# Retention attention and two feed-forward stages on one core: other ways to spread 1/rms, column sums and two scalars, one table row moved, and the last store halved

## The chip, the core and the metric

The program runs on one core of a Trainium2 chip. The core has TensorE (PE, matrix products into PSUM), VectorE (DVE), ScalarE (ACT), GpSimd (POOL) and SyncE (SP, which here only issues DMAs). The metric is the device time of one execution, in microseconds. The kernel before took 584.2 us as the median of three runs (584.07 to 584.91).

## The reference

Three stages follow one another on 1536 tokens of 512 channels, all in float32:

```python
# 1: causal retention in 8 heads of 64 channels, decay lam[h], two sequences of 768 tokens
out = ((q k^T) * lam^(i-j)) v, carried from block to block in a 64x64 state
# 2: x (1536x512) -> h = x @ w_in (512x2048)
r = maximum(h, 0); g = s * r * r + b; x = g @ w_out        # w_out 2048x512, s and b are scalars
# 3: rms = sqrt(mean(x*x, axis=-1) + 1e-6); xn = x / rms * rms_g
g = xn @ w_gate; val = xn @ w_val                          # 512x1536 each
out = (silu(g) * val) @ w_out                              # 1536x512
```

## The kernel before

**Layout.** Tokens lie along the free dimension, in two blocks of 768 (s = 0 and 1, `BW`), channels on the 128 partitions. A float32 product is made of three products of rounded parts (`PASSES`: high by high, high by low, low by high); ACT writes a high part (L143) and DVE the low part, source minus high (L146).

**Order.** The order of each engine's instructions is the order of the code (`manual_schedule`): generators `hquad` and `quad` yield after each part of a unit, and a table `plan`, keyed by (unit, part), says which other work is issued there. Semaphores hold an instruction until its inputs are there, and an engine does not pass a waiting instruction.

**Stage 2, h.** Sixteen units, `hquad(0)` to `hquad(15)`. From unit 4 on a unit is seven products of six matmuls (a 2x2 scheme with seven products instead of eight), in four PSUM banks b0 to b3; units take turns with two sets of banks. The parts are: product into b0, ACT copies it out (L378); product into b1, DVE adds (L316); product into b2, DVE adds; product into b3, DVE adds; and last three more products that are accumulated onto b0, b2 and b3, each of which therefore waits until the earlier reader of its bank is done. In between, `w_tasks` prepares the weights of later units from raw words: `first` to `fourth` unpack (ACT L123 and L129, DVE shift L135 and sum L140) and POOL makes four sums (L220 to L223); `first_hi`, `first_lo`, `second_hi`, `second_lo` split them. The table rows `wt[6]` and `wt[7]` say in which parts of units 9 to 12 this is done.

**Stage 2, second product.** For each block 16 steps of a `y_product` (512 tokens, four channel groups, 12 matmuls) and a `z_product` (256 tokens, 12 matmuls). The bias b enters as b times the column sums of w_out: POOL adds the rows of w_out into `wsum` (L434), and in step 15 of block 0 TensorE sums `wsum` over partitions and spreads s and b from one row, both with plain float32 products into bank 3 (L864, L865). DVE makes `sg_col`, `bc_col`, `bg_col` from that (L866 to L869); ACT (`square`) and DVE (`take`) then read y and z out with them.

**1/rms.** `norm_rstd(s)` sums squares over channels with TensorE (`nps`, L766), DVE scales (L768), POOL takes the power -1/2 (L770) and splits the 128x6 result in two parts (L773, L774). `norm_apply` spreads it: 12 products of 128 columns whose weights are a column of a part repeated (L781) give a bank `rb` in which every partition holds 1/rms of its token, and `norm_scale` multiplies x by that (DVE, L795). For block 0 this stands in steps 1, 3 and 4 of block 1's y products, for block 1 in quads 0 and 1.

**Stage 3.** 24 units `quad(0)` to `quad(23)` like `hquad`, with ACT's Silu (L982, L989) and a product on DVE (L958); quads 0 to 3 are of block 0. Then `out_product` and `store`: 12 row tiles, copied out of PSUM by ACT (even) or DVE (odd) and sent by SP.

## Time and profile before

| | |
|---|---|
| median of three runs | 584.2 us (584.07 to 584.91) |
| the profiled execution | 584.34 us, span 582.6 us |
| granted TensorE clock | 0.999 |
| busy: PE, DVE, ACT, POOL | 575.9, 404.4, 319.9, 114.6 us |
| the chain that ended last | 95% PE, 2% DMA, 1% DVE, 1% ACT |
| stages on TensorE | attention to 43.6, h to 165.8, y and z to 303.4, quads to 481.0, out to 579.0 us |

Times in rows are microseconds from the first instruction of the profiled execution. A busy figure of PE includes the pipelined ends of matmuls, so the distance from one group's start to the next one's start is read as its cost. A bracket at a row's end gives the idle time before it on its engine and what ended it.

### The profile page before, as it was taken

To read this page: it belongs to the slowest core of one execution; us is meant where nothing else is said; L and a number is where in the kernel's file an instruction comes from. 1 tells how busy PE (TensorE), PEld (TensorE's weight loads), DVE (VectorE), ACT (ScalarE), POOL (GpSimd) and SP (SyncE) were. 2 spreads that over 40 slices of the span, in tenths; PEclk is the share of its full clock that TensorE was granted. 3 is DMA by queue.
4 is the path that set the end of the run, shared out by engine and by line. 5 is a ranking of instruction groups with operands and counts; after the bars stand their busy time and mean duration, and the time that the engine had idled before them with its cause. 6 is when DMAs were issued, how large, how long until landed. Compare 5 with 4: busy or idle time off the path is not lost.

```text
span 582.6 us, 9398 instructions
## 1 busy us (share of the span) xinstructions
PE 575.9 (99%) x3682; PEld 536.8 (92%) x3682; DVE 404.4 (69%) x642; ACT 319.9 (55%) x558; POOL 114.6 (20%) x129
## 2 busy tenths in 40 slices
PE   8999999999999999999999999999999999999997
PEld 7889999999998888888899999999999998888886
DVE  6688947777777774769847967777777777874200
ACT  3889977776876662537552434444444446763200
POOL 4660312212123330222211002222222200000000
PEclk9999999999999999999999999999999999999999
DMA  8972222222324330222110012222222213320300
GB/s 327 397 291 75 72 74 73 73 74 72 109 73 145 123 131 1 73 72 71 30 45 2 1 37 61 75 72 75 71 75 75 79 36 109 108 73 1 146 36 37
DMA packets 17283, 52.00 MB, mean 89 GB/s; under 512 B 2390, under 2 KB 2390, under 8 KB 17238
## 3 DMA queue, kind: packets, MB, share of 16 engines
q1 hardware_dynamic: 17232, 51.39, 25.7%
q8 instruction: 29, 0.48, 0.3%
q14 instruction: 16, 0.13, 0.1%
q10 hardware_dynamic: 6, 0.00, 0.0%
HBM read 48.24 MB, written 3.15 MB: 88 GB/s over the span
## 4 chain that ended last, share of the span: by engine, by line
PE 95%; DMA 2%; DVE 1%; ACT 1%; SPq 0%; issue 0%; DVEq 0%
PE q L305 30%; PE h L305 20%; PE out L1095 17%; PE y L806 15%; PE z L818 8%; PE o L581 2%; PE sc L527 2%; DMA k<-in_kT_dram 1%; DMA q<-in_qT_dram 1%; PE o L596 1%; PE st L591 1%; PE rb L781 0%; PE nps L766 0%; DVE u_None L140 0%; DVE u_None L135 0%; DVE xq_None L316 0%
## 5 line engine op out<-in xcount | busy, mean ns | idle before, releaser
L143 ACT ACTIVATE u_None<-u_None 128x768 fp32r<-128x768 f32 (+2 forms) x50 | 42.8, 870 | 51.8 <-DVE u_None L140 45.8
L305 PE MATMUL q<-u0b_None,u_None 128*128 128x384 f32 x360 | 68.0, 334 | 0.0
L305 PEld LDWEIGHTS q<-u0b_None,u_None 128*128 128x128 f32 x360 | 62.7, 188 | 0.0
L146 DVE TENSOR_TENSOR u_None<-u_None,u_None 128x512 fp32r<-128x512 f32 (+1 forms) x66 | 53.1, 829 | 11.1 <-ACT u_None L143 11.0
L220 POOL TENSOR_TENSOR u_None<-u_None 128x256 f32<-128x256 f32 x18 | 19.8, 1099 | 184.4 <-DVE u_None L140 184.4
L305 PE MATMUL q<-xs_None,u_None 128*128 128x384 f32 x288 | 55.2, 334 | 0.0
L123 ACT ACTIVATE u_None<-st_None 128x512 f32<-128x512 f32 x68 | 45.1, 664 | 17.6 <-issue 14.3
L140 DVE CUSTOM_DVE_ANT_0 u_None<-u_None 128x1024 uint16<-128x1024 uint16 x68 | 47.1, 693 | 5.7 <-ACT u_None L129 0.6
L305 PEld LDWEIGHTS q<-xs_None,u_None 128*128 128x128 f32 x288 | 50.4, 188 | 0.0
L129 ACT ACTIVATE u_None<-st_None 128x512 uint32<-128x512 uint16 x68 | 45.2, 664 | 5.1 <-DVE u_None L146 5.1
L316 DVE TENSOR_TENSOR st_None<-q,r_None 128x384 f32<-128x384 f32 x48 | 26.6, 554 | 19.1 <-PE q L305 19.1
L989 ACT ACTIVATE st_None<-r_None 128x384 f32<-128x384 f32 x24 | 12.6, 526 | 45.9 <-DVE r_None L316 43.3
L1095 PE MATMUL out<-u_None,xs_None 128*128 128x512 f32 x144 | 32.8, 389 | 0.0
L1095 PEld LDWEIGHTS out<-u_None,xs_None 128*128 128x128 f32 x144 | 27.0, 188 | 5.6
L135 DVE TENSOR_SCALAR u_None<-u_None 128x512 uint32<-128x512 uint32 x68 | 31.1, 457 | 1.2 <-ACT u_None L123 1.0
L1102 DVE COPY st_None<-out 128x512 f32<-128x512 f32 x4 | 2.8, 692 | 40.9 <-PE out L1095 40.9
L434 POOL TENSOR_TENSOR wsum_None<-wsum_None,u_None 128x512 f32<-128x512 f32 x15 | 20.6, 1373 | 47.8 <-DVE u_None L140 47.8
L305 PE MATMUL q<-u0a_None,u_None 128*128 128x384 f32 x144 | 28.8, 334 | 0.0
L305 PE MATMUL q<-g_None,u_None 128*128 128x384 f32 x144 | 26.9, 334 | 0.0
L1095 PE MATMUL out<-u_None,u0b_None 128*128 128x512 f32 x108 | 25.3, 389 | 0.0
L305 PEld LDWEIGHTS q<-u0a_None,u_None 128*128 128x128 f32 x144 | 25.3, 188 | 0.0
L305 PEld LDWEIGHTS q<-g_None,u_None 128*128 128x128 f32 x144 | 25.1, 188 | 0.0
(207 smaller groups left out, 1291.9 us busy)
## 6 DMA issues: line engine op xcount, KB each, us to landing
st_None<-in_w_dram SPq DMA_DIRECT2D x68, 512.0 KB, 3.3
kv<-in_kv_dram SPq DMA_DIRECT2D x12, 512.0 KB, 7.2
q<-in_qT_dram SPq DMA_DIRECT2D x12, 256.0 KB, 7.1
k<-in_kT_dram SPq DMA_DIRECT2D x12, 256.0 KB, 7.1
out_dram<-st_None SPq DMA_DIRECT2D x8, 256.0 KB, 2.0
out_dram<-u_None SPq DMA_DIRECT2D x4, 256.0 KB, 2.0
row<-in_lam_dram ACTq DMA_DIRECT2D x1, 0.0 KB
row<-in_s_dram ACTq DMA_DIRECT2D x1, 0.0 KB
```

Source lines behind the costliest of these rows:

```text
L123: nc.scalar.activation(m, t[:, :, 1].bitcast(F32), AF.Prelu, scale=2.0**-112, alpha=-(2.0**32))
L129: nc.scalar.activation(to.bitcast(U32), low, AF.Copy, scale=2.0**-13)
L135: nc.vector.tensor_scalar(m, m, 3, None, op0=ALU.logical_shift_left)
L140: nc.vector.tensor_tensor(m, m, t.bitcast(U32), op=ALU.add)
L143: nc.scalar.activation(to, src, AF.Copy)
L146: nc.vector.tensor_tensor(to, src, hi.bitcast(F32), op=ALU.subtract)
L305: nc.tensor.matmul(ps, ws[:, wi, wop * KC + kt * P : wop * KC + (kt + 1) * P], xs[xop][:, xi, kt, :], start=n == 0 and not more, stop=n == ...
L316: nc.vector.tensor_tensor(to, ps, more, op=ALU.add)
L434: nc.gpsimd.tensor_tensor(wsum, wsum, m, op=ALU.add)
L806: nc.tensor.matmul(acc[d], wt[:, wi, d * P : (d + 1) * P], gt[:, gi, 0:BT], start=it == 0 and pi == 0, stop=it == NF1 - 1 and pi == 2,)
L818: nc.tensor.matmul(acc2[d // 2][:, d % 2 * BX : (d % 2 + 1) * BX], wt[:, wi, d * P : (d + 1) * P], gt[:, gi, BT:BW], start=it == 0 and pi ...
L1095: nc.tensor.matmul(ps, rows_[:, ai], w_out[f][:, wi, :], start=first and pi == 0, stop=last and pi == 2)
```

## The change

- **Column sums of w_out.** `wsum` is split in two parts in step 13 of block 0 (ACT, DVE), two products of 512 columns with a matrix of ones (`ones_r`, made once by POOL) put the sums in bank 3 behind the z products of that step, ACT copies one row out of PSUM, and two DMAs on SP's queue take it to DRAM and back as 128x4 (`cs_col`), 512 pieces of 4 bytes. DVE reads that in step 15, behind the products.
- **s and b** are loaded by two DMAs on SP's queue that repeat the one value over 128 partitions, behind `g_col`'s; the two DMAs on ACT's queue and the small product go.
- **1/rms of block 0** goes to DRAM as one row (a DMA of 768 pieces of 4 bytes) and comes back repeated over 128 partitions into `m_r`, both on SP's queue; `norm_scale` reads SBUF. The 12 products go.
- **1/rms of block 1.** ACT (high part) and POOL (low part) multiply the unit matrix by 1/rms, which gives diagonal matrices of two tiles each; a product of `ones_r` and a diagonal spreads it. Six products of 256 columns in place of twelve of 128, in quad 1, and six scalings in place of four.
- **One unit of h** (`wt[6]`, and the first task of `wt[7]`) in other slots.
- **The last row tile** is stored in halves: ACT copies and sends one, DVE copies and SP sends the other.

In the table the rows of `wt[6]` and `wt[7]` change; the diff cut to its core:

```diff
+                nc.sync.dma_start(s_col, s.partition_broadcast(P))
+                nc.sync.dma_start(b_col, b.partition_broadcast(P))
+    ones_r = late.tile([P, P], F32R, name="ones_r")
+    nc.gpsimd.tensor_copy(ones_r, ones)
...
-        (wt[6], ((9, 4), (10, 1), (10, 2), (10, 2), (10, 3), (10, 4), (10, 4), (11, 0))),
-        (wt[7], ((11, 1), (11, 3), (11, 4), (11, 4), (12, 1), (12, 2), (12, 2), (12, 3))),
+        (wt[6], ((9, 4), (10, 1), (10, 2), (10, 3), (10, 3), (10, 4), (11, 0), (11, 1))),
+        (wt[7], ((11, 2), (11, 3), (11, 4), (11, 4), (12, 1), (12, 2), (12, 2), (12, 3))),
...
+        return rstd
+
+    def spread_by_memory(rstd):
+
+        row = dram.tile([BW], F32, name="rstd_row")
+        nc.sync.dma_start(row.rearrange("(t p) -> p t", p=P), rstd)
+        nc.sync.dma_start(m_r, row.partition_broadcast(P))
...
+    def diagonals(rstd):
+
+        parts = const.tile([P, 2, NTT], F32R, name="parts")
+        nc.gpsimd.tensor_copy(parts[:, 0], rstd)
+        nc.gpsimd.tensor_tensor(parts[:, 1], rstd, parts[:, 0].bitcast(F32), op=ALU.subtract)
+        for n in range(NTT // 2):
+            hi, lo = rooms[n % 2]
+            for t in range(2):
+                nc.scalar.activation(
+                    hi[:, t * P : (t + 1) * P], unit, AF.Copy, scale=parts[:, 0, 2 * n + t : 2 * n + t + 1].bitcast(F32)
+                )
+            nc.gpsimd.tensor_tensor(
+                lo.rearrange("p (t i) -> p t i", t=2),
+                unit.rearrange("p (o i) -> p o i", o=1).to_broadcast([P, 2, P]),
+                parts[:, 1, 2 * n : 2 * n + 2].bitcast(F32).rearrange("p (t o) -> p t o", o=1).to_broadcast([P, 2, P]),
+                op=ALU.mult,
+            )
+            yield hi, lo
+
+    def norm_apply(s, n, ps, d):
+
+        for i in range(2):
+            nc.tensor.matmul(ps[:, 0 : 2 * P], ones_r, d[i], start=i == 0, stop=i == 1)
+        norm_scale(s, slice(2 * n * P, 2 * (n + 1) * P), ps[:, 0 : 2 * P])
...
+            if m == NF1 - 3:
+                split_hi(wsum_parts[0], wsum)
+                split_lo(wsum_parts[1], wsum, wsum_parts[0])
...
+            if m == NF1 - 3:
+
+                cs = bank(3, "cs")
+                for i in range(2):
+                    nc.tensor.matmul(cs, ones_r, wsum_parts[i], start=i == 0, stop=i == 1)
+                nc.scalar.activation(wsum[0:1, :], cs[0:1, :], AF.Copy)
+                row = dram.tile([1, DM], F32, name="cs_row")
+                nc.sync.dma_start(row, wsum[0:1, :])
+                nc.sync.dma_start(cs_col, row.rearrange("o (d p) -> p (o d)", p=P))
+            if m == NF1 - 1:
+                nc.vector.tensor_scalar(sg_col, g_col, s_col, None, op0=ALU.mult)
+                nc.vector.tensor_scalar(bc_col, cs_col, b_col, None, op0=ALU.mult)
+                nc.vector.tensor_tensor(bg_col, bc_col, g_col, op=ALU.mult)
...
-                norm_rstd(0, bank(0, "nps0"))
+                spread_by_memory(norm_rstd(0, bank(0, "nps0")))
             if it in (3, 4):
-                h = it - 3
-                norm_apply(0, slice(h * HB, (h + 1) * HB), bank(1 - h, f"rb0_{h}")[:, 0:HB])()
+                cols = slice((it - 3) * HB, (it - 2) * HB)
+                norm_scale(0, cols, m_r[:, cols])
...
         product(b0, ws, xs, A12, B21, True)
+        while between:
+            between.pop()()
...
+    rows_of = {}
+
+    def rstd_1():
+        d = diagonals(norm_rstd(1, bank(1, "nps1")))
+        rows_of.update(zip(range(2), d))
+        rows_of[None] = d
+
+    def spread(n):
+        norm_apply(1, n, bank((2, 3, 1)[n], f"rb1_{n}"), rows_of[n])
...
-        (0, 4): [lambda: norm_rstd(1, bank(1, "nps1"))],
-        (1, 2): [spread],
-        (1, 3): [lambda: scale[1]()],
+        (0, 4): [rstd_1],
+        (1, 3): [
+            lambda: spread(0), lambda: spread(1), lambda: rows_of.update({2: next(rows_of[None])}),
+            lambda: between.append(lambda: spread(2)),
+        ],
...
+        if i == NT // P - 1:
+
+            for j, (buf, queue) in enumerate(((out_buf[0], nc.scalar), (to, nc.sync))):
+                c = slice(j * DM // 2, (j + 1) * DM // 2)
+                if j:
+                    nc.vector.tensor_copy(buf[:, c], ps[:, c])
+                else:
+                    nc.scalar.activation(buf[:, c], ps[:, c], AF.Copy)
+                queue.dma_start(out[i * P : (i + 1) * P, c], buf[:, c])
+            return
```

Three places where instructions stand elsewhere now. First VectorE in units 10 and 11 of h, before: `h_2`, `h_3` and `h_1` in a row are banks b2, b3 and b1 of a unit, L135 and L140 are the shift and the sum of the raw words, L146 the low parts.

```order
L316 TENSOR_TENSOR xq_5_None<-h_2_1527,r_None 128x384
L135 TENSOR_SCALAR u_2_None<-u_2_None 128x512
L140 ISA u_2_None<-u_2_None 128x1024
L316 TENSOR_TENSOR xq_5_None<-h_3_1528,xq_5_None 128x384
L316 TENSOR_TENSOR xq_5_None<-h_2_1527,r_None 128x384
L316 TENSOR_TENSOR xq_5_None<-h_3_1528,r_None 128x384
L405 TENSOR_SCALAR xq_5_None<-xq_5_None 128x384
L146 TENSOR_TENSOR u_3_None<-u_2_None,u_3_None 128x768
L146 TENSOR_TENSOR u_3_None<-u_2_None,u_3_None 128x512 x2
L316 TENSOR_TENSOR r_None<-h_1_1597,q_9_None 128x384
L316 TENSOR_TENSOR u_17_None<-h_2_1598,r_None 128x384
L316 TENSOR_TENSOR u_17_None<-h_3_1599,u_17_None 128x384
```

The same place now:

```order
L315 TENSOR_TENSOR xq_5_None<-h_2_1528,r_None 128x384
L135 TENSOR_SCALAR u_2_None<-u_2_None 128x512
L315 TENSOR_TENSOR xq_5_None<-h_3_1529,xq_5_None 128x384
L140 ISA u_2_None<-u_2_None 128x1024
L315 TENSOR_TENSOR xq_5_None<-h_2_1528,r_None 128x384
L315 TENSOR_TENSOR xq_5_None<-h_3_1529,r_None 128x384
L404 TENSOR_SCALAR xq_5_None<-xq_5_None 128x384
L146 TENSOR_TENSOR u_3_None<-u_2_None,u_3_None 128x768
L315 TENSOR_TENSOR r_None<-h_1_1597,q_9_None 128x384
L146 TENSOR_TENSOR u_3_None<-u_2_None,u_3_None 128x512 x2
L315 TENSOR_TENSOR u_17_None<-h_2_1598,r_None 128x384
L315 TENSOR_TENSOR u_17_None<-h_3_1599,u_17_None 128x384
```

The second sum stands behind the add that reads b3 of unit 10, and the pair of low parts (`second_lo`) has gone from ahead of the add that reads b1 of unit 11 to the place between it and the add that reads b2.

Second ScalarE at the turn from quad 0 to quad 1, before: `q_0_3046` is b0 of quad 0, `q_0_3120` b0 of quad 1; the copy of b0 (L967), its Silu (L982) and the Silu of the other half (L989).

```order
L982 ACTIVATE st_24_None<-q_0_3046 128x384
L989 ACTIVATE st_24_None<-r_None 128x384
L967 ACTIVATE st_24_None<-q_0_3120 128x384
L982 ACTIVATE st_24_None<-q_0_3120 128x384
L989 ACTIVATE st_24_None<-r_None 128x384
L143 ACTIVATE xs_None<-xq_6_None 128x768
```

The same place now, where L996 is the copy, L1013 and L1020 the two Silu:

```order
L1013 ACTIVATE st_24_None<-q_0_3038 128x384
L1020 ACTIVATE st_24_None<-r_None 128x384
L798 ACTIVATE wsum_None<-unit_r,parts 128x128 x2
L798 ACTIVATE u_22_None<-unit_r,parts 128x128 x2
L996 ACTIVATE st_24_None<-q_0_3119 128x384
L798 ACTIVATE wsum_None<-unit_r,parts 128x128 x2
L1013 ACTIVATE st_24_None<-q_0_3119 128x384
L1020 ACTIVATE st_24_None<-r_None 128x384
L143 ACTIVATE xs_None<-xq_6_None 128x768
```

Four of ACT's multiplications of the unit matrix stand ahead of the copy of quad 1's b0, and two behind it.

Third VectorE in quad 1, before: L316 are the adds, L146 low parts of weights, L795 the scalings of x.

```order
L316 TENSOR_TENSOR r_None<-q_1_3121,st_24_None 128x384
L146 TENSOR_TENSOR u_23_None<-u_2_None,u_23_None 128x512 x2
L316 TENSOR_TENSOR st_24_None<-q_2_3122,r_None 128x384
L795 TENSOR_TENSOR xq_6_None<-xq_6_None,rb_0_3149 128x2x384 x2
L316 TENSOR_TENSOR st_24_None<-q_3_3123,st_24_None 128x384
L795 TENSOR_TENSOR xq_6_None<-xq_6_None,rb_1_3156 128x2x384 x2
L316 TENSOR_TENSOR st_24_None<-q_2_3122,r_None 128x384
L316 TENSOR_TENSOR r_None<-q_3_3123,r_None 128x384
```

The same place now, with the scalings in L784:

```order
L315 TENSOR_TENSOR r_None<-q_1_3120,st_24_None 128x384
L146 TENSOR_TENSOR u_23_None<-u_2_None,u_23_None 128x512 x2
L315 TENSOR_TENSOR st_24_None<-q_2_3121,r_None 128x384
L315 TENSOR_TENSOR st_24_None<-q_3_3122,st_24_None 128x384
L784 TENSOR_TENSOR xq_6_None<-xq_6_None,rb_0_3155 128x2x256 x2
L784 TENSOR_TENSOR xq_6_None<-xq_6_None,rb_1_3160 128x2x256 x2
L784 TENSOR_TENSOR xq_6_None<-xq_6_None,rb_2_3174 128x2x256 x2
L315 TENSOR_TENSOR st_24_None<-q_2_3121,r_None 128x384
L315 TENSOR_TENSOR r_None<-q_3_3122,r_None 128x384
```

All scalings stand behind the add that reads b3 and ahead of the add that reads b2 for the second time (the last row but one shown starts with `st_24_None<-q_2`).

## Rows read from the trace of the kernel before

**Rows 1.** the page, part 4: shares of the chain that ended last.

```profile
PE 95%; DMA 2%; DVE 1%; ACT 1%; SPq 0%; issue 0%; DVEq 0%
```

**Rows 2.** stretch: PE, PEld, DVE, ACT, POOL busy us (instructions); clock, DMA share, GB/s.

```profile
317.00:324.00 7.00, 7.00 (x43) 7.00 (x42) 6.86 (x11) 2.13 (x4) 0.00 (x0) 1.00 0.00 1
```

**Rows 3.** the chain of waits: start us, us, what.

```profile
227.10 1.43 PE z L818 x12
229.63 2.94 PE y L806 x12
...
250.66 1.43 PE z L818 x12
252.70 2.80 PE y L806 x12
...
315.35 1.29 PE rb L781 x12
```

**Rows 4.** POOL timeline, 214 to 262: start us, us, instruction, idle before and releaser.

```profile
243.88 1.46 POOL L770 TENSOR_TENSOR rstd<-ms,neg_half 128x6 f32<-128x6 f32 x1 [24.43 <-DVE ms L768]
```

**Rows 5.** DMA issues: what, KB each, median us from issue to landing.

```profile
st_None<-in_w_dram SPq DMA_DIRECT2D x68, 512.0 KB, 3.3
...
g_col<-in_rms_g_dram SPq DMA_DIRECT2D x1, 2.0 KB, 4.9
```

**Rows 6.** TensorE timeline, 104 to 146.

```profile
126.17 1.25 PE L305 MATMUL h<-u0a_None,st_None 128*128 128x384 f32 x6
128.09 1.32 PE L305 MATMUL h<-u0b_None,st_None 128*128 128x384 f32 x6 [0.67 <-DVE xq_None L316]
129.25 1.21 PE L305 MATMUL h<-xs_None,st_None 128*128 128x384 f32 x6
...
134.46 1.20 PE L305 MATMUL h<-wm_None,st_None 128*128 128x384 f32 x6
```

**Rows 7.** VectorE timeline, 104 to 146.

```profile
125.96 0.78 DVE L135 TENSOR_SCALAR u_None<-u_None 128x512 uint32<-128x512 uint32 x1
126.88 0.69 DVE L140 CUSTOM_DVE_ANT_0 u_None<-u_None 128x1024 uint16<-128x1024 uint16 x1
```

**Rows 8.** ScalarE timeline, 104 to 146.

```profile
127.60 0.85 ACT L143 ACTIVATE u_None<-u_None 128x768 fp32r<-128x768 f32 x1 [1.82 <-DVE u_None L140]
...
130.34 1.04 ACT L143 ACTIVATE u_None<-u_None 128x1024 fp32r<-128x1024 f32 x1
131.29 0.47 ACT L378 ACTIVATE q_None<-h 128x384 f32<-128x384 f32 x1
...
132.40 0.66 ACT L123 ACTIVATE u_None<-st_None 128x512 f32<-128x512 f32 x1
```

**Rows 9.** POOL timeline, 296 to 336.

```profile
314.46 0.19 POOL L773 CAST parts<-rstd 128x6 fp32r<-128x6 f32 x1
```

**Rows 10.** ScalarE groups by shape: count, busy us, mean ns, idle before.

```profile
L550 ACT ACTIVATE kdec<-kv,dec 128x64 f32<-128x64 f32 x40 | 10.6, 336 | 7.1 <-DMA kv<-in_kv_dram 7.0
...
L603 ACT ACTIVATE xq_None<-o 128x256 f32<-128x256 f32 x12 | 4.4, 370 | 3.1 <-PE o L596 3.1
```

**Rows 11.** VectorE timeline, 296 to 336.

```profile
314.42 0.56 DVE L316 TENSOR_TENSOR r_None<-q,st_None 128x384 f32<-128x384 f32 x1 [1.23 <-PE q L305]
314.89 1.28 DVE L146 TENSOR_TENSOR u_None<-u_None,u_None 128x512 fp32r<-128x512 f32 x2
...
321.13 0.56 DVE L316 TENSOR_TENSOR r_None<-q,r_None 128x384 f32<-128x384 f32 x1
...
326.13 0.55 DVE L316 TENSOR_TENSOR st_None<-q,st_None 128x384 f32<-128x384 f32 x1
```

**Rows 12.** POOL timeline, 104 to 146.

```profile
125.72 0.74 POOL L220 TENSOR_TENSOR u_None<-u_None 128x256 f32<-128x256 f32 x1 [10.24 <-DVE u_None L140]
```

**Rows 13.** TensorE timeline, 326 to 372.

```profile
326.94 3.28 PE L305 MATMUL q<-u0b_None,u_None 128*128 128x384 f32 x18
```

**Rows 14.** VectorE timeline, 540 to 584.

```profile
579.02 0.69 DVE L1102 COPY st_None<-out 128x512 f32<-128x512 f32 x1 [15.63 <-PE out L1095]
```

More of the change, by code (lines that the diff above doesn't have):

```diff
@@ L150, in attention_moe_moe2_kernel @@
     params = const.tile([P, H], F32, name="params")
-    row2 = const.tile([1, 2], F32, name="row2")
     params2 = const.tile([P, 2], F32, name="params2")
@@ L759, in norm_total @@
         norm_pair(s, 0)
-    rstd_parts = {}
+    dram = ctx.enter_context(tc.tile_pool(name="dram", bufs=1, space=bass.MemoryType.DRAM))
     def norm_rstd(s, ps):
@@ L795, in norm_scale @@
             nc.vector.tensor_tensor(y, y, by, op=ALU.mult)
+    def diagonals(rstd):
+        parts = const.tile([P, 2, NTT], F32R, name="parts")
+        nc.gpsimd.tensor_copy(parts[:, 0], rstd)
+        nc.gpsimd.tensor_tensor(parts[:, 1], rstd, parts[:, 0].bitcast(F32), op=ALU.subtract)
+        room = piece(early, "wsum", 2)
+        rooms = [[at(room, i, 1) for i in range(2)], [at(m_late[t], 14, 1) for t in ("u4", "u5")]]
+        unit = unit_r.bitcast(F32)
+        out = []
+        for n in range(NTT // 2):
[15 more added lines that the diff above has]
+        norm_scale(s, slice(2 * n * P, 2 * (n + 1) * P), ps[:, 0 : 2 * P])
     ops2 = []
+    wsum_parts = [at(t, 12, 2) for t in (m_u2, m_st1)]
+    cs_col = const.tile([P, NK], F32, name="cs_col")
     for blk in range(B):
@@ L860, in attention_moe_moe2_kernel @@
             r_hi(m + 3)
-            if m == NF1 - 1:
-                cs = bank(3, "cs")
-                for d in range(NK):
-                    nc.tensor.matmul(cs[:, d : d + 1], wsum[:, d * P : (d + 1) * P], ones[:, 0:1], start=True, stop=True)
-                nc.tensor.matmul(cs[:, NK : NK + 2], ones[0:1, :], row2, start=True, stop=True)
-                nc.vector.tensor_copy(params2, cs[:, NK : NK + 2])
-                nc.vector.tensor_scalar(sg_col, g_col, s_col, None, op0=ALU.mult)
-                nc.vector.tensor_scalar(bc_col, cs[:, 0:NK], b_col, None, op0=ALU.mult)
-                nc.vector.tensor_tensor(bg_col, bc_col, g_col, op=ALU.mult)
+            if m == NF1 - 3:
+                split_hi(wsum_parts[0], wsum)
+                split_lo(wsum_parts[1], wsum, wsum_parts[0])
             for d in range(NK):
@@ L958, in a_mult @@
             nc.vector.tensor_tensor(a_at[order[q]], v_both, silu, op=ALU.mult)
+    between = []
     def quad(i):
@@ L1047, in attention_moe_moe2_kernel @@
     xt = x_tasks(xq[1], ops2[1], xq[0])
-    scale = []
-    def spread():
-        for h in range(2):
-            scale.append(norm_apply(1, slice(h * HB, (h + 1) * HB), bank(2 + h, f"rb1_{h}")[:, 0:HB]))
-        scale[0]()
+    rows_of = {}
[5 more added lines that the diff above has]
+        norm_apply(1, n, bank((2, 3, 1)[n], f"rb1_{n}"), rows_of[n])
     plan = {
```

22 lines of the change are left out of this document (2 added, 20 removed).

## The prediction

> **What bounds the kernel now.** I read the page's chain first: 95% of what ended last is TensorE [rows 1], so only time that TensorE loses or is spared counts. Next the busy time by stretch: in quads 1 and 2 VectorE works 6.86 us of 7.00 [rows 2], so there whatever puts VectorE back also puts TensorE back, shortly after. Then the chain in order of time, for what the removed products cost; then the timelines around units 10 and 11 of h and around quads 1 and 2. Times are on the clock of the profiled execution.
>
> **Column sums, s and b.** The z products of step 14 end at 227.10 + 1.43 = 228.53; y of step 15 starts at 229.63 and takes 2.94 for twelve products against 2.80 in a later step [rows 3]. So the plain float32 products cost 1.10 + 0.14 = 1.24. Two products of 512 columns replace them, at 2.80 / 12 = 0.23 each: 0.47. Saved 0.77. Their operands are made two steps earlier on ACT and DVE, whose queues have room there. The trip through DRAM: the products follow the z products of step 13, one step of 4.2 ahead of 228.53, and end at 224.8; ACT's copy out of PSUM (0.6 for its 512 columns, from the 0.37 for 256 [rows 10]) ends at 225.4. VectorE and ACT have until about 232 to begin with y and z of block 0 before block 1 wants their banks, by my count of the 0.7 to 0.8 that each of these reads takes. g_col, the same shape, landed 4.9 after its issue, behind other loads [rows 5]; a load of 512 KB takes 3.3 [rows 5]. With 3.3 for the store and 3.3 to 4.9 for the load it is 232.1 to 233.7 at worst, with 2 and 3 it is 230.5. I take no loss; the bound is 1.5. The two issues for s and b sit on SP's queue some 190 us ahead of their use: nothing.
>
> **1/rms of block 0.** The z products end at 250.66 + 1.43 = 252.09 and y starts at 252.70 [rows 3]: 0.61 for six products, and a second six one step later. Removed: 1.22. The power is ready at 243.88 + 1.46 = 245.34 [rows 4]. The row goes out in 768 pieces; at g_col's rate, 4.9 for 512 [rows 5], that is 7.35, so 252.7; the load back, 3.3 like a weight load [rows 5], ends at 256.0. Who waits: VectorE, at the first scaling (252.7 before), and behind it the low part for step 6. Without the twelve products step 6 starts about 260.3; two scalings and the low part take 2.7, so the row may land until 257.5. Cover 1.5, loss 0. SP also holds the next weight load behind both DMAs, some 10 us later than now; ACT then waits one or two microseconds for it, in a stretch where it idles for longer. Bounds: 0 and 3.
>
> **One unit of h.** TensorE stands for 0.67 ahead of the last product of unit 10 until an add on b3 is done [rows 6]. A product takes (134.46 - 129.25) / 5 = 1.04, so 128.09 could be 126.17 + 1.04 = 127.21. VectorE's shift ends at 126.74 and the sum follows at 126.88 [rows 7]; now the add comes first, ends near 127.2, and the product starts about 127.26: 0.83 won, and unit 11 starts at 128.42. But ACT's `first_hi` waits for the sum, which is now later: 127.84 for 127.60. From there the copy of unit 11's b0 takes the place that `second_hi` had, 2.74 on [rows 8]: 130.58. `second_hi` comes behind it and a square, 1.11 on (131.29 to 132.40 [rows 8]), at 131.69, and takes 1.04: 132.73. VectorE holds the pair `second_lo` for it, ahead of the add that reads b2. The pair takes 1.2 (1.28 less the overlap with the next row [rows 11]), the add 0.55: 134.5. TensorE wants to accumulate on b2 at 128.42 + 5.21 = 133.63. It stands 0.93, and the first group after a stand takes 0.12 more (1.16 for 1.04). Net: 1.05 - 0.83 = 0.22 lost. The stall moves one unit on and grows a little. Bounds: 0.83 won (no wait in unit 11) and 0.5 lost.
>
> **1/rms of block 1.** The twelve products cost 1.29 [rows 3]; six of 256 columns at 1.43 / 12 = 0.12 cost 0.72. But ACT must make four diagonals before it copies quad 1's b0. The parts are there at 314.46 + 0.19 = 314.65 [rows 9]. A 128x128 multiplication with a scale per partition is not in the trace; the nearest row is 128x64 with such a scale, 0.336 [rows 10], and 128x256 without takes 0.37 [rows 10]. I take 0.3 from one start to the next: 315.9; the copy adds 0.47 [rows 8]: 316.35. VectorE's add on b1, at 314.42 before [rows 11], starts at 316.37, 1.95 later, and VectorE has idled that long. Then the pair L146 (1.2 from start to start [rows 11]). POOL's third product starts as soon as TensorE has read the first diagonal, about 316.7, beside this pair. A POOL sum takes 0.74 [rows 12], and the shift that began 0.24 into it lasted 0.78 and ended 0.28 after it [rows 7]: VectorE and POOL hold each other up. I take 0.6 for it, bounds 0 and 0.74. (The Trainium skill, "SBUF — State Buffer", section "Who interferes with whom", says that a VectorE instruction with two SBUF inputs and a GpSimd instruction that reads SBUF share a port, and the second waits for the whole of the first. By that the pair would start 0.58 late, and the sum would be the same; the row is of a one-input shift, so no row here shows it for this pair.) So 316.37 + 0.47 + 1.2 + 0.6 = 318.64; two adds at 0.47: 319.58; six scalings of 512 at 0.60, as the halves of the L146 pair: 323.18; an add, and the add that stood at 321.13 [rows 11] comes at 323.65, 2.52 later. All behind it on VectorE shifts by that, since it has no idle time there [rows 2]. The fourth add of quad 2 (326.13 [rows 11]) ends at 326.13 + 2.52 + 0.55 = 329.20, and TensorE's last product of quad 2, at 326.94 [rows 13], waits for it: 2.26 later. That already holds the 1.29 - 0.72 = 0.57 that the products spare. So a gain of 0.57 turns into a loss of 2.26. Bounds: 0.57 won (VectorE catches up) and 3 lost (ACT at 0.37 for each diagonal, POOL at its full hold-up).
>
> **The last tile.** VectorE's copy takes 0.69 at the very end [rows 14]. ACT's half takes 0.37 (128x256 out of PSUM [rows 10]), VectorE's half 0.35 to 0.5. In the changed program VectorE's half waits for ACT's, as both read one bank: 0.37 + 0.03 + 0.42 = 0.82, 0.13 later, less a little for a DMA of half the size. I take +0.1, bounds -0.3 and +0.3.
>
> **Sum.** -0.77 - 1.22 + 0.22 + 2.26 + 0.1 = +0.6, on 584.34 (the profiled execution, span 582.6 and 1.74 around it), which is 0.14 above the median of 584.2. Forecast: 584.8.
>
> **Rivals.**
> *A, the products are simply spared.* VectorE's late start in quad 1 is caught up before TensorE needs its banks: for it, quad 1's own waits have more than 2 us of room; against it, VectorE's 6.86 of 7.00 in the next stretch [rows 2]. Then 2.26 becomes -0.57: 584.2 - 0.77 - 1.22 + 0.22 - 0.57 + 0.1 = 582.0; if unit 11 of h does not wait either, 580.9.
> *B, the row through DRAM is late.* Place: VectorE's first scaling of block 0. It decides from a landing at 257.5, 12.2 after the power. At g_col's rate there is room of 1.5; if a piece of 4 bytes takes twice as long to write as g_col's took to read, 245.34 + 14.7 + 3.3 = 263.3, 5.8 late, and the low parts for steps 6 and 7 with it: 584.8 + 5.8 = 590.6. For it: 768 pieces; against it: g_col's 4.9 was measured behind two weight loads, so its own rate is better. (The Trainium skill, "DMA: Bandwidth & Descriptors", section "Rules for kernel authors", says that a DMA with a strided last dimension becomes one descriptor per element, and that a DMA that reads what another wrote must wait for its completion. The code has both; how long they take no run here shows.)
>
> **Chances.** Forecast 0.66, A 0.22, B 0.07, others on the slow side (the row for the column sums late, ACT slower) 0.05. Measurement tells about 0.2% here, 1.2 us: below 583.0 is faster, above 585.4 slower. The forecast's own range by its bounds is 583.4 to 586.0; I put 0.47 of its 0.66 within the 1.2 and 0.18 above. Faster 0.23, same 0.47, slower 0.30. The range that holds it 8 times in 10 takes in A's first figure and stops short of B: 582.0 to 586.2.
>
> **What would show it.** No gap on TensorE at 228.5 and after the z products of steps 18 and 19 of the y stage; the first product of step 6 not idle. In h the idle time of 0.67 ahead of unit 10's last product gone, and one of about 0.9 ahead of unit 11's product onto b2, with `second_lo` as its cause. ACT's four multiplications ahead of the copy in quad 1, VectorE idle for about 3 us there, and TensorE waiting for scalings or adds in quads 1 and 2, 2 to 3 us in all. If TensorE has no idle time in quads 1 and 2, the largest term is wrong and A has come; if a wait of VectorE for a DMA of over 5 us stands ahead of the first scaling of block 0, B has.

## The result and the profile of the changed kernel

The changed kernel took **591.27 us** (median of six runs, 590.12 to 592.68) against 584.86 for the kernel before in the same comparison: a ratio of 1.0111, 95% interval 1.0094 to 1.0128. The forecast was 584.8, range 582.0 to 586.2. The profiled execution of the changed kernel took 590.12 us, with a span of 588.32 for the 582.57 of the kernel before, so 5.75 us of span are to be found. (The medians lie 6.4 apart; the other 0.7 is in neither profile.)

Where they are is read from where TensorE's stages begin. The start of h alone moves by 1.7 us between profiles (43.1 to 44.8 over the kernels here, which share the code of the attention stage), so lengths of stages are compared, not clock times. "Block 1" here runs from the sum of squares of block 0 (`nps`) to the first product of quad 0.

| length on TensorE, us | h | y, z to `nps` | block 1 | quads | out, to its last products |
|---|---|---|---|---|---|
| before | 122.14 | 76.55 | 61.23 | 177.42 | 97.28 |
| after | 122.42 | 75.71 | 65.29 | 179.88 | 97.29 |
| difference | +0.28 | -0.84 | **+4.06** | **+2.46** | +0.01 |
| the prediction's term | +0.22 | -0.77 | -1.22 | +2.26 | (tail) +0.1 |

With -0.30 at the start and +0.09 in the tail that is 5.76, the 5.75 but for rounding. Four of the five terms came within 0.2 us. The term for 1/rms of block 0 was wrong by 5.3.

The chain by engine shows in one line that something has changed: what was 95% PE in [rows 1] is now shared with VectorE and DMAs.

```profile
PE 82%; DVE 8%; DMA 5%; ACT 2%; POOL 1%; issue 1%; ACTq 0%; DVEq 0%; POOLq 0%; SPq 0%
```

**Block 0's row.** The timeline of the changed kernel from 243 to 270, all engines (start, duration, instruction; in the bracket the idle time before it and what ended that):

```profile
243.02 1.46 POOL L771 TENSOR_TENSOR rstd<-ms,neg_half 128x6 f32<-128x6 f32 x1 [23.56 <-DVE ms L769]
...
244.51 0.37 SPq L777 DMA_DIRECT2D rstd_row<-rstd  x1
...
253.89 0.32 SPq L778 DMA_DIRECT2D r_None<-rstd_row  x1
254.31 9.06 SPq L116 DMA_DIRECT2D st_None<-in_w_dram  x3
...
259.83 1.83 DVE L784 TENSOR_TENSOR xq_None<-xq_None,r_None 128x768 f32<-128x768 f32 x2 [8.42 <-DMA r_None<-rstd_row]
...
261.05 0.67 ACT L123 ACTIVATE u_None<-st_None 128x512 f32<-128x512 f32 x1 [9.11 <-DMA st_None<-in_w_dram]
...
261.58 0.95 DVE L146 TENSOR_TENSOR st_None<-u_None,st_None 128x768 fp32r<-128x768 f32 x1
...
262.58 4.15 PE L826 MATMUL y<-st_None,u0b_None 128*128 128x512 f32 x11 [2.76 <-DVE st_None L146]
```

One more wait of TensorE stands at the end of the stage (TensorE, 290 to 298):

```profile
295.58 0.73 PE L826 MATMUL y<-st_None,g_None 128*128 128x512 f32 x2 [0.52 <-DVE st_None L146]
```

The write is issued as soon as the power is there ([rows 4] for before) and the read back can only be issued 9.4 later. VectorE's first scaling stands 8.42 for that read, the low part (L146) follows the scaling, and TensorE stands 2.76 for the low part. ScalarE stands too, 9.11, for a weight load that was queued behind both DMAs. Which of these costs the time a trace can't say: the experiments do. From 262 to 296 VectorE works 31.45 of 34.00 us, and 27.63 in the same stretch before (windows; columns as in [rows 2]):

```profile
262.00:296.00 34.00, 32.90 (x176) 28.42 (x177) 31.45 (x39) 20.14 (x28) 9.00 (x8) 0.95 0.15 48
```

The list of DMAs has the two landings (last column: us from issue to landing):

```profile
r_None<-rstd_row SPq DMA_DIRECT2D x1, 384.0 KB, 5.9
...
rstd_row<-rstd SPq DMA_DIRECT2D x1, 3.0 KB, 9.3
```

Most of these two times is no moving of data. The last two columns of the windows are the DMA engines' busy share and the GB/s that they moved:

```profile
244.50:246.00 1.50, 1.50 (x10) 1.30 (x9) 0.59 (x2) 1.22 (x2) 1.42 (x2) 1.00 0.24 2
246.00:253.90 7.90, 7.90 (x46) 6.92 (x45) 3.69 (x4) 3.29 (x5) 2.99 (x3) 1.00 0.00 0
253.90:256.80 2.90, 2.90 (x20) 2.64 (x19) 0.00 (x0) 0.00 (x0) 0.00 (x0) 1.00 0.00 0
256.80:259.80 3.00, 3.00 (x19) 2.47 (x18) 0.00 (x0) 0.00 (x0) 0.00 (x0) 1.00 0.65 254
```

The 3 KB of the write have moved by 246.0, and its landing is reported 7.8 later; the read, issued at 253.89, moves nothing before 256.8.

**Block 1's diagonals.** The timeline of the changed kernel in quads 1 and 2, which answers to [rows 9] and [rows 11]:

```profile
317.65 0.19 POOL L789 CAST parts<-rstd 128x6 fp32r<-128x6 f32 x1
317.88 0.70 ACT L798 ACTIVATE wsum_None<-unit_r,parts 128x128 fp32r<-128x128 f32 x2 [2.64 <-POOL parts L789]
...
319.06 0.47 ACT L996 ACTIVATE st_None<-q 128x384 f32<-128x384 f32 x1
...
319.57 0.56 DVE L315 TENSOR_TENSOR r_None<-q,st_None 128x384 f32<-128x384 f32 x1 [3.18 <-ACT st_None L996]
...
322.19 1.31 PE L304 MATMUL q<-u0a_None,u_None 128*128 128x384 f32 x6 [0.85 <-DVE st_None L315]
...
326.53 1.30 PE L304 MATMUL q<-u0b_None,u_None 128*128 128x384 f32 x6 [0.95 <-DVE xq_None L784]
```

ScalarE stands 2.64 for POOL's parts, with the copy of quad 1's b0 (L996) behind the diagonals; VectorE stands 3.18 for that copy where it stood 1.23 before, and TensorE then waits 0.85 and 0.95 for VectorE.

**The unit of h.** TensorE, ScalarE and VectorE in units 10 and 11, against [rows 6 to 8]:

```profile
126.95 1.32 PE L304 MATMUL h<-u0b_None,st_None 128*128 128x384 f32 x6
...
131.38 1.04 ACT L143 ACTIVATE u_None<-u_None 128x1024 fp32r<-128x1024 f32 x1
...
132.46 1.29 DVE L146 TENSOR_TENSOR u_None<-u_None,u_None 128x512 fp32r<-128x512 f32 x2 [1.12 <-ACT u_None L143]
...
134.28 1.31 PE L304 MATMUL h<-wm_None,st_None 128*128 128x384 f32 x6 [0.81 <-DVE u_None L315]
```

The wait of 0.67 in unit 10 is gone; one of 0.81 stands in unit 11, and VectorE held `second_lo` ahead of the add, as predicted.

**The rest.** The timeline of the changed kernel at the turn to step 15 of block 0, and at its end:

```profile
228.80 0.23 DVE L899 TENSOR_SCALAR bc_col<-cs_col,params 128x4 f32<-128x4 f32 x1 [1.50 <-DMA cs_col<-cs_row]
228.81 2.91 PE L826 MATMUL y<-st_None,u0b_None 128*128 128x512 f32 x12
...
584.73 0.38 ACT L1144 ACTIVATE st_None<-out 128x256 f32<-128x256 f32 x1 [7.56 <-PE out L1131]
...
585.15 0.42 DVE L1142 COPY st_None<-out 128x256 f32<-128x256 f32 x1 [16.09 <-ACT st_None L1144]
```

VectorE stands 1.50 for the column sums and TensorE doesn't stand at all. At the end VectorE's half waits for ScalarE's, 0.84 in all for the 0.69 of [rows 14].

### The profile page after: what moved, and what is told of

Its sections match the earlier page's. It is cut to its first block, busy times and chain, and to the rows that moved or that the text cites. A ratio compares the mean times of both kernels' runs of the same rounds, so it can differ in the third digit from the quotient of the medians.

```text
span 588.3 us, 9367 instructions
## 1 busy us (share of the span) xinstructions
PE 577.1 (98%) x3656; PEld 535.8 (91%) x3656; DVE 405.9 (69%) x644; ACT 323.4 (55%) x567; POOL 117.9 (20%) x131
## 4 chain that ended last, share of the span: by engine, by line
PE 82%; DVE 8%; DMA 5%; ACT 2%; POOL 1%; issue 1%; ACTq 0%; DVEq 0%; POOLq 0%; SPq 0%
PE q L304 28%; PE h L304 18%; PE out L1131 17%; PE y L826 10%; PE z L838 5%; DMA rstd_row<-rstd 2%; PE sc L524 1%; DVE u_None L146 1%; DVE xq_None L784 1%; PE o L578 1%; DMA k<-in_kT_dram 1%; DMA q<-in_qT_dram 1%; DMA r_None<-rstd_row 1%; DVE u0b_None L146 1%; DVE st_None L146 1%
## 5 line engine op out<-in xcount | busy, mean ns | idle before, releaser
L143 ACT ACTIVATE u_None<-u_None 128x768 fp32r<-128x768 f32 (+2 forms) x50 | 42.9, 871 | 50.1 <-DVE u_None L140 44.8
L146 DVE TENSOR_TENSOR u_None<-u_None,u_None 128x512 fp32r<-128x512 f32 (+1 forms) x66 | 54.4, 849 | 11.4 <-ACT u_None L143 11.4
L140 DVE CUSTOM_DVE_ANT_0 u_None<-u_None 128x1024 uint16<-128x1024 uint16 x68 | 47.1, 693 | 5.9 <-ACT u_None L129 0.9
L1020 ACT ACTIVATE st_None<-r_None 128x384 f32<-128x384 f32 x24 | 12.6, 526 | 49.0 <-DVE r_None L315 49.0
L135 DVE TENSOR_SCALAR u_None<-u_None 128x512 uint32<-128x512 uint32 x68 | 31.0, 456 | 1.4 <-ACT u_None L123 1.0
L1131 PEld LDWEIGHTS out<-u_None,u0b_None 128*128 128x128 f32 x108 | 20.3, 188 | 4.2
```

What stands on the lines that cost most here:

```text
L135: nc.vector.tensor_scalar(m, m, 3, None, op0=ALU.logical_shift_left)
L140: nc.vector.tensor_tensor(m, m, t.bitcast(U32), op=ALU.add)
L143: nc.scalar.activation(to, src, AF.Copy)
L146: nc.vector.tensor_tensor(to, src, hi.bitcast(F32), op=ALU.subtract)
L1131: nc.tensor.matmul(ps, rows_[:, ai], w_out[f][:, wi, :], start=first and pi == 0, stop=last and pi == 2)
```

## The experiments

Theory 1 for block 0: VectorE waits for the row, and TensorE for VectorE. Theory 2, its rival: the weight load that stands behind the row on SP's queue is what costs. For block 1: ScalarE's diagonals hold the copy and so VectorE, against products or POOL as the cause.

All are compared with the kernel before on the same chip. The lengths of the two stages in dispute and the start of block 0's first scaling are from the profile of each:

| run | median us | ratio to before (95%) | block 1 | quads | first scaling, us after `nps` |
|---|---|---|---|---|---|
| after | 591.27 | 1.0111 (1.0094 to 1.0128) | 65.29 | 179.88 | 18.48 |
| a1 products in block 0 | 586.86 | 1.0040 (1.0027 to 1.0053) | 61.21 | 179.91 | - |
| a2 products in block 1 | 587.48 | 1.0052 (1.0039 to 1.0065) | 64.67 | 177.42 | 17.90 |
| a3 low parts late | 589.88 | 1.0096 (1.0082 to 1.0110) | 64.93 | 179.89 | 18.14 |
| b1 weight load first | 590.99 | 1.0114 (1.0100 to 1.0128) | 64.61 | 179.91 | 17.80 |
| b2 row unread | 586.30 | 1.0043 (1.0029 to 1.0056) | 61.21 | 179.89 | - |
| b3 row transposed | 586.48 | 1.0035 (1.0022 to 1.0049) | 60.08 | 179.91 | 10.73 |
| b4 diagonals behind | 588.57 | 1.0071 (1.0059 to 1.0084) | 64.75 | 178.00 | 17.95 |
| d1 row one step later | 588.07 | 1.0057 (1.0044 to 1.0071) | 62.54 | 179.91 | 15.74 |
| c1 three mended | 583.91 | 0.9989 (0.9980 to 0.9998) | 60.08 | 178.02 | 10.87 |
| c2 products in block 1 | 582.76 | 0.9968 (0.9957 to 0.9979) | 60.10 | 177.42 | 10.92 |

**a1, block 0 by products again.**

```diff
...
-                spread_by_memory(norm_rstd(0, bank(0, "nps0")))
+                parts0 = row_parts(norm_rstd(0, bank(0, "nps0")))
...
-                norm_scale(0, cols, m_r[:, cols])
+                ps = bank(4 - it, f"rb0_{it}")[:, 0:HB]
+                row_products(parts0, cols, ps)
+                norm_scale(0, cols, ps)
```

> The changed kernel with one part undone: 1/rms of block 0 is spread by twelve products again, no row goes through DRAM. Theory 1 (the row lands 2.8 us too late, TensorE stands for it and then runs some microseconds at a lower granted clock; stands and clock together about 5.3, less the 1.2 of the products): about 587.2 us, and no wait of TensorE at step 6 of block 1's y products. Rival (block 0 costs little and the time went with block 1 and the last tile): above 590. If it is 587.2, what is left over the kernel before is +2.4: block 1 +2.5, h +0.3, tail 0, column sums -0.65, start -0.3.

Measured 586.86; block 1 is 61.21, the length it had before, with no wait of TensorE in it. So the whole +4.06 belongs to the row. That settles where the time goes, not yet how.

**a2, block 1 by products again.**

```diff
...
-        (1, 3): [
-            lambda: spread(0), lambda: spread(1), lambda: rows_of.update({2: next(rows_of[None])}),
-            lambda: between.append(lambda: spread(2)),
-        ],
+        (1, 2): [spread],
+        (1, 3): [lambda: norm_scale(1, slice(HB, BW), rows_of[1])],
```

> The changed kernel with 1/rms of block 1 spread by twelve products of 128 columns again instead of diagonals. Theory 1 (ACT's four diagonals ahead of the copy of quad 1's b0 put a saturated VectorE back): about 588.8 us, 2.5 less than the changed kernel, and VectorE's idle time ahead of quad 1's add on b1 back from 3.2 to about 1.2 us. Rival (VectorE catches up, the diagonals only spare products): 0.6 more, 591.9 us.

Measured 587.48. The quads are 177.42 long, as before, 2.46 less than in the changed kernel and as expected. The median is 1.3 below the expected one; of that the profile shows 0.62 in block 1, where the row happened to land earlier. VectorE's idle time is 1.23 again:

```profile
317.72 0.56 DVE L315 TENSOR_TENSOR r_None<-q,st_None 128x384 f32<-128x384 f32 x1 [1.23 <-PE q L304]
```

**a3, `second_lo` two parts later.** The pair then stands behind the task that unpacks the next unit's words, so this unit's low parts are made of other words; the number and the sizes of the instructions are those of the changed kernel.

```diff
-        (wt[6], ((9, 4), (10, 1), (10, 2), (10, 3), (10, 3), (10, 4), (11, 0), (11, 1))),
+        (wt[6], ((9, 4), (10, 1), (10, 2), (10, 3), (10, 3), (10, 4), (11, 0), (11, 3))),
```

> The changed kernel with the pair second_lo of one unit of h issued two parts later (in part 3 of unit 11 instead of part 1), behind the add that reads b2. Theory 1 (VectorE holds that add behind the pair, which waits for ACT): TensorE's wait of 0.81 us ahead of unit 11's product onto b2 goes, 0.8 to 1.0 us faster, about 590.4 us. Rival (the wait moves to the later adds of unit 11 or to the product that needs the low parts): no change within 0.3 us.

The wait of 0.81 went, and h is 122.32 long for 122.42: the rival has it. In TensorE's timeline one wait less in unit 11 stands against a new one in unit 12:

```profile
133.24 1.20 PE L304 MATMUL h<-wm_None,st_None 128*128 128x384 f32 x6
...
140.61 1.32 PE L304 MATMUL h<-u0a_None,u_None 128*128 128x384 f32 x6
142.34 1.32 PE L304 MATMUL h<-u0b_None,u_None 128*128 128x384 f32 x6 [0.41 <-DVE xq_None L315]
```

142.34 is 1.73 behind 140.61, where six matmuls take 1.04. (Of the 1.4 between the medians the profiles show 0.36 in block 1, where the row landed earlier, and not the rest.)

**a4, the transfers by themselves.** Added at the end of the changed kernel, each waiting for the one before:

```diff
...
+            row = dram.tile([BW], F32, name="probe")
+            for n in (1, 3, 6):
+                nc.sync.dma_start(row[0 : n * P].rearrange("(t p) -> p t", p=P), last_rstd[0][:, 0:n])
+            nc.sync.dma_start(row.rearrange("(o t) -> o t", o=1), m_r[0:1, :].bitcast(F32))
+            nc.sync.dma_start(row.rearrange("(a t) -> a t", a=6), m_r[0:6, 0:P].bitcast(F32))
+            nc.sync.dma_start(m_r, row.partition_broadcast(P))
```

> The changed kernel with six DMAs one after the other at its end, all onto one DRAM row: 128, 384 and 768 pieces of 4 bytes from 128 partitions, the same 3 KB from one partition, the same from six partitions, and the row read back over 128 partitions. Its time is longer by these. Theory 1 (the number of 4-byte pieces sets the 9.3 us of the row's write): landings of about 3, 5.5 and 9 us, and 2 to 3 us for the one and for the six pieces. Rival (a fixed cost of going to DRAM, or the queue's other loads): the three lie within 1.5 us of one another, at 2 to 4 us with nothing beside them, or all near 9. The read back of 384 KB: 3 to 4 us with nothing beside it, against 5.9 beside a weight load.

The list of DMAs (last column: us from issue to landing) and SP's queue:

```profile
probe<-rstd SPq DMA_DIRECT2D x1, 0.5 KB, 7.4
probe<-rstd SPq DMA_DIRECT2D x1, 1.5 KB, 10.2
probe<-rstd SPq DMA_DIRECT2D x1, 3.0 KB, 10.9
```

```profile
614.05 0.24 SPq L1152 DMA_DIRECT2D probe<-r_None  x1
615.25 0.28 SPq L1153 DMA_DIRECT2D probe<-r_None  x1
616.44 0.35 SPq L1154 DMA_DIRECT2D r_None<-probe  x1
```

The 3 KB take 10.9 as 768 pieces and 1.2 as one piece or as six (615.25 - 614.05, 616.44 - 615.25). So the small pieces cost it, but not in proportion: 128 of them already take 7.4 (beside the last output stores), three times as many 2.8 more, six times as many 3.5 more. My 7.35, a rate times a count, was of the wrong form: in the trace the pieces of all three have moved 1.2 to 1.4 after the issue, and the rest, 6.2 to 9.5, is the wait for the report that they have landed. The three also differ from the one piece and the six in that they leave from 128 partitions, but that alone doesn't cost it: an output store leaves from 128 partitions too, in pieces of 2 KB, and lands after 2.0. (The execution took 622.42 with the transfers.) The read back, behind the six pieces, ended with the span, at 620.6, so it took 4.2 at most with nothing beside it.

**b1 and b2, the weight load.** b1 (first diff, against the changed kernel) puts the load ahead of the row; b2 (second diff, against a1) puts the row's DMAs into a1 with nobody reading the row.

```diff
             work(1)
+            if it == 1:
+                spread_by_memory(rstd0)
             r_lo(m + 3)
```

```diff
-                parts0 = row_parts(norm_rstd(0, bank(0, "nps0")))
+                rstd0 = norm_rstd(0, bank(0, "nps0"))
+                spread_by_memory(rstd0)
+                parts0 = row_parts(rstd0)
```

> The changed kernel with block 0's two row DMAs issued behind the first work of step 1, so the weight load that stood behind them on SP's queue goes ahead of them (at about 240 instead of 254.3). Theory 1 (VectorE's first scaling waits for the row, and the low part for step 6 is behind it): the row still lands at 258 to 259.5, the wait ahead of step 6 is 1.3 to 2.5 us instead of 2.8; 1.5 to 2.5 us faster than the changed kernel, 588.8 to 589.8. Theory 2 (the weight load held back 14 us is what costs): the wait ahead of step 6 goes, at or below 587.5 us. In both ScalarE's idle time of 9.1 us ahead of its unpacking goes.

> The kernel with block 0's 1/rms spread by products (run a1), and the two row DMAs put back where the changed kernel has them, with nobody reading the row: only the weight load is held back behind them. Theory 1 alone: as a1, 586.9 within 0.4. Theory 2: ScalarE's unpacking comes 8 us late, VectorE stands at the shift behind it, the low part for step 7 comes at about 266.5, and TensorE waits 1.5 to 3 us there or later: 588.4 to 589.9.

b1: 590.99, nothing gained. ScalarE's idle time of 9.1 went, but the row landed hardly earlier in the stage (17.80 after `nps`; 17.90 to 18.48 in after, a2, a3 and b4): its read took 6.1 for 5.9, with two weight loads issued 0.4 and 0.9 behind it as in the changed kernel, and began to move data as late, 2.8 after its issue for 3.0. b2: 586.30, block 1 61.21, as a1, although ScalarE and VectorE both stood for the held load:

```profile
260.72 0.66 ACT L123 ACTIVATE u_None<-st_None 128x512 f32<-128x512 f32 x1 [8.37 <-DMA st_None<-in_w_dram]
...
261.42 0.43 DVE L135 TENSOR_SCALAR u_None<-u_None 128x512 uint32<-128x512 uint32 x1 [2.81 <-ACT u_None L123]
```

Theory 2 falls: the held load costs nothing that TensorE sees. Theory 1 missed in b1 as well, by 1.2 us at least: I had expected the read to be shorter with the load out of its way.

**b3, the row turned first.** Two products with the unit matrix turn the 128x6 result into 6x128, ScalarE copies it out, and six pieces of 512 bytes go to DRAM.

```diff
...
+        for i in range(2):
+            nc.tensor.matmul(ps, parts[:, i], unit_r, start=i == 0, stop=i == 1)
+        rows = wsum[0:NTT, 0:P]
+        nc.scalar.activation(rows, ps, AF.Copy)
+        row = dram.tile([BW], F32, name="rstd_row")
+        nc.sync.dma_start(row.rearrange("(t p) -> t p", p=P), rows)
+        nc.sync.dma_start(m_r, row.partition_broadcast(P))
...
+            if it == 2:
+                spread_transposed(parts0, bank(1, "tr0")[0:NTT, 0:P])
```

> The changed kernel with block 0's 1/rms turned by two products into six rows of 128 before it goes to DRAM, so the write is six pieces of 512 bytes in place of 768 of 4; it is issued in step 2, behind the weight load. If the small pieces are the cause: write 1.2 to 2 us (as in the probe) in place of 9.3, the row lands at about 253 to 254.5, no wait of TensorE at step 6, block 1's y stage 60.2 (61.21 before, less 1.22, plus 0.25): about 585.9 us, 1.0 below a1. If the trip to DRAM and back itself is the cause, or VectorE is held anyway by the read from SBUF: a wait remains and it is 587 or more.

```profile
246.89 0.28 PE L784 MATMUL tr<-unit_r,parts 128*6 128x128 f32 x2
...
247.50 0.28 SPq L788 DMA_DIRECT2D rstd_row<-wsum_None  x1
...
248.74 0.33 SPq L789 DMA_DIRECT2D r_None<-rstd_row  x1
...
252.11 1.83 DVE L801 TENSOR_TENSOR xq_None<-xq_None,r_None 128x768 f32<-128x768 f32 x2 [0.34 <-DMA r_None<-rstd_row]
```

Written in 1.24, back in 3.3, no wait of TensorE, block 1 60.08 as expected: 1.15 less than before. The profiled execution took 584.9, the median was 586.48, 0.6 more than expected. So the trip as such was not the fault, and with large pieces it pays in the stage: 60.08 to 60.10 in b3, c1 and c2, 61.21 to 61.23 with products (before, a1, b2). The medians don't resolve that gain: b3 is 2.3 above its kernel before, a1 2.1 above its own. (The Trainium skill, "DMA: Bandwidth & Descriptors", section "Specifications", says that transfers below 512 bytes become a read, a change and a write. The runs agree in kind, 8.4 to 9.3 us for the pieces of 4 bytes in the kernels and 1.2 for those of 512; they don't show the mechanism.)

The read back is shorter here for two reasons, and the loads beside it are the smaller one. In d1, below, two weight loads were issued 0.4 and 1.7 behind the read, and it took 4.2 (windows of d1, the read issued at 254.06):

```profile
254.05:255.00 0.95, 0.95 (x6) 0.78 (x5) 0.00 (x0) 0.95 (x2) 0.00 (x0) 1.00 0.00 0
255.00:258.20 3.20, 3.20 (x21) 2.88 (x20) 0.00 (x0) 0.75 (x2) 0.00 (x0) 1.00 0.79 242
```

Data move from 1.0 after the issue on. So they do in b3, c1, c2 and the last read of a4 too, all behind a write of six pieces; behind the 768 pieces (after, a2, a3, a4, b1, b2, b4) they begin 2.6 to 3.0 after the issue. Of the 2.56 by which the changed kernel's read is longer than b3's, 2.04 is this late start, and 0.52 is left for the loads beside it. The late start goes with the small pieces in all twelve reads; why, no run here shows.

**d1, b3 with the row one step later.** Here the row lands 15.7 after `nps`, 1.9 later than the prediction had it and 0.4 past the room that it gave it.

```diff
-            if it == 2:
+            if it == 3:
                 spread_transposed(parts0, bank(1, "tr0")[0:NTT, 0:P])
```

> Run b3 with the two products that turn the row, and so its trip through DRAM, one step later: the row lands at about 256 to 257.5, which is where the prediction saw it and inside the room to 257.5 that the prediction gave it. If VectorE's queue from the first scaling to the quads paces the stage (in six runs the quads began 46.77 to 46.81 us after that scaling, with the clock lowered or not), the stage is the landing plus 46.8, 1.4 to 3 us longer than b3's 60.08: 587.5 to 589.5 us. If the room was as predicted, up to the low part for step 6, there is no wait and it is as b3, 586.5 within 0.6.

```profile
258.26 1.83 DVE L801 TENSOR_TENSOR xq_None<-xq_None,r_None 128x768 f32<-128x768 f32 x2 [5.34 <-DMA r_None<-rstd_row]
...
265.66 2.81 PE L843 MATMUL y<-st_None,xs_None 128*128 128x512 f32 x11 [0.17 <-DVE st_None L146]
...
293.99 0.73 PE L843 MATMUL y<-st_None,g_None 128*128 128x512 f32 x2 [1.36 <-DVE st_None L146]
```

588.07 us, block 1 62.54: 2.46 more than b3. There is no wait at step 6, for which the prediction reckoned its room, and TensorE is 0.1 behind b3 there. By step 8 it is 0.8 behind, and 1.65 more is lost 36 us after the scaling, at the stage's last low part. Quad 0 starts at 305.06, 46.80 after the first scaling. In after, a2, a3, a4, b1 and b4 that distance is 46.81, 46.77, 46.79, 46.79, 46.81 and 46.80. From that scaling on VectorE's queue is what sets the end of the stage. (It isn't VectorE alone: the chain of the changed kernel runs from the scaling to the last low part, which ends at 295.5, with 2.8 us of POOL's sums and 2.7 of ScalarE's high parts in it, made from what VectorE had just written.) So every 0.1 us that the row lands later is paid in full, and it is free only up to 60.08 - 46.80 = 13.3 after `nps` (worked out, not run).

**b4, diagonals behind the copy.**

```diff
...
-        rows_of.update(zip(range(2), d))
...
+        (1, 0): [lambda: rows_of.update(zip(range(2), rows_of[None]))],
```

> The changed kernel with the first two pairs of diagonals issued behind ScalarE's copy of quad 1's b0 instead of ahead of it. Theory 1 (the copy, and by it VectorE, is held): VectorE's idle time ahead of quad 1's add on b1 back from 3.2 to 1.2 us, TensorE's waits of 0.85, 0.95 and 0.21 in quads 1 and 2 down to 0.5 in all or less, the quads 177.0 to 177.4 us in place of 179.9: 2.5 to 2.9 us faster, about 588.6. Rival (six scalings in a row behind the add on b3, or POOL's products beside VectorE, are what delays): 1 us or less of the 2.5 comes back, 590.3 or more.

588.57, and the quads are 178.00: 1.88 of the 2.46 come back, where I expected 2.5 or more. VectorE's idle time is 1.23 again. A part of what remains is to be seen at the pair and at POOL:

```profile
318.54 1.70 DVE L146 TENSOR_TENSOR u_None<-u_None,u_None 128x512 fp32r<-128x512 f32 x2
318.65 1.04 POOL L801 TENSOR_TENSOR wsum_None<-unit_r,parts 128x256 fp32r<-128x256 f32 x1
...
319.14 1.10 DVE L146 TENSOR_TENSOR u_None<-u_None,u_None 128x512 fp32r<-128x512 f32 x1
...
320.76 0.38 PE L812 MATMUL rb<-u_None,ones_r 128*128 128x256 f32 x1 [0.38 <-POOL u_None L801]
```

The pair takes 1.70 for 1.28 [rows 11], POOL's product 1.04 for 0.62 in the changed kernel: each is held up by the other by 0.42, and TensorE waits 0.38 for POOL's second diagonal. (The third row is the second half of the pair by itself.) The order is a turn each: the first half of the pair takes its usual 0.68; POOL's product, issued 0.11 after it, is 0.42 longer; the second half, issued while that runs, is 0.42 longer (1.10); POOL's second product, issued while that runs, is 0.44 longer. The add that reads b3 for the second time comes 0.75 later in quad 1 than before: 0.42 is the pair, and 0.33 is left for the six scalings in a row, which no run here takes apart. (The Trainium skill, "SBUF — State Buffer", section "Who interferes with whom", has it that of two such instructions the second waits for the whole of the first. The trace agrees: each held instruction is longer by what was left of the one ahead of it, to 0.15.)

**c1 and c2, what is left when the faults are mended.** c1 is b3 and b4 together, with the unit of h changed only in its second sum; c2 is c1 with twelve products in block 1.

```diff
-        (wt[6], ((9, 4), (10, 1), (10, 2), (10, 3), (10, 3), (10, 4), (11, 0), (11, 1))),
-        (wt[7], ((11, 2), (11, 3), (11, 4), (11, 4), (12, 1), (12, 2), (12, 2), (12, 3))),
+        (wt[6], ((9, 4), (10, 1), (10, 2), (10, 3), (10, 3), (10, 4), (10, 4), (11, 0))),
+        (wt[7], ((11, 1), (11, 3), (11, 4), (11, 4), (12, 1), (12, 2), (12, 2), (12, 3))),
...
```

> The changed kernel with three things mended: block 0's row turned before it goes to DRAM (as in b3), the diagonals of block 1 behind ScalarE's copy (as in b4), and of the unit of h only the second sum one part later (its second_hi and second_lo stay where the kernel before has them). From the profiles: b3 584.9, quads 178.0 in place of 179.9, h 122.0 in place of 122.4 (wait of 0.81 ahead of unit 11's product onto b2 down to about 0.45): 582.6 us, 0.3% below the kernel before. If the waits only move on in VectorE's full stretches, 584 or more.

> As c1, but 1/rms of block 1 by twelve products as in the kernel before (quads 177.4). 582.0 us, 0.5 below c1, the fastest so far, 0.4% below the kernel before: column sums -0.65, block 0's row -1.15, h -0.1, start and tail 0 to -0.3. If c1 is the faster one, the diagonals pay once VectorE is not late when they come.

c1 583.91, c2 582.76 with the kernel before at 584.52: ratios 0.9989 and 0.9968. h is 121.97 and 121.99 long (122.14 before), with a wait of 0.36 in unit 11 in place of 0.81. c2 is faster than the kernel before by 0.3%, 0.4% expected; c1 by 0.1%, 0.3% expected. Both are 0.8 to 1.3 us above the times I wrote down, which I had worked out from b3's profiled execution, its fastest. Part of c1's lies outside the span: its executions last 1.7 to 2.8 longer than their spans (median 2.1), those of c2 and of the kernel before 1.7 to 1.9; what it is no run shows. By the median span c1 is 0.2% below the kernel before. The diagonals do not pay even when the copy is not held: 178.02 against 177.42.

## Why the prediction was wrong

**Column sums: right.** -0.84 for -0.77. The load back landed in 2.1 where I had allowed up to 4.9, and VectorE's wait for it lay beside TensorE's work.

**1/rms of block 0: wrong, and it decided.** The failed step is "so the row may land until 257.5. Cover 1.5, loss 0". It failed in both numbers. Counted from `nps` (242.21 in the kernel before) the prediction had the row landing at 13.8 and room to 15.3. It landed at 18.5, because the steps "that is 7.35" and "the load back, 3.3 like a weight load" were both short: the write took 9.4 and the read 5.9, of which 3.0 passed before it moved any data. And the room ended at 13.3, because I reckoned it to the first instruction behind the scaling that TensorE needs, the low part for step 6, instead of to the end of VectorE's queue. 18.5 - 13.3 = 5.2, which with 1.15 spared is the +4.06. The predicted landing itself would have cost 0.5 (worked out), and d1, at 15.7, only 0.4 past the room as predicted, cost 2.46. Rival B was this mechanism at the right place; it put the time at 590.6 and its chance at 0.07. The chance was far too small, and the price was good in part by luck: it had the row landing 21.1 after `nps`, 2.6 too late, and the room ending at 15.3, 2.0 too late, and the two errors nearly cancel (5.8 late for 5.2).

**The weight load held behind the row: half right.** I let ScalarE wait one or two microseconds and cost it at nothing. It waits 9.1, and b2 shows that nothing is right.

**Unit of h: right**, +0.28 for +0.22, by the mechanism named. (The stand that it put at 0.93 is 0.87 by its own terms, 134.5 - 133.63; 0.81 was measured.) a3 shows that the wait can't simply be moved off the pair; c2 shows that leaving the second half of the old order alone gains 0.15 on before.

**1/rms of block 1: right**, +2.46 for +2.26. VectorE's add on b1 came 1.96 late in quad 1 for 1.95, the pair was held up by POOL by 0.35 for 0.6, and the add behind the scalings came 2.63 late for 2.52. b4 parts it: 1.88 is ScalarE's order; 0.58 stays when that is mended, although the products themselves are shorter: POOL's turns with VectorE are the part that the trace shows. Rival A would have needed the diagonals free.

**The last tile: right**, +0.09 for +0.1.

## What to carry to other kernels

Reckon the room for a late result to the end of the queue of the engine that waits for it, not to the next instruction that another engine needs: here an engine with 31.45 us of work in 34 gave nothing back, and the wait shows up tens of microseconds later under another name. Before sending a small result through DRAM, turn it so that it leaves in large pieces (512 bytes here), since with the pieces of 4 bytes both the write's landing and the start of the read behind it were late, and look at what else is queued beside the read back. Work that an in-order engine does ahead of the copy that frees another engine is paid by that other engine.
